# Weight split without a float32 copy, narrower packed operands, and a shorter key norm in a delta-attention and two-FFN kernel

## Chip, core and metric

The kernel runs on one core of a Trainium2 chip. The metric is the device time of one execution in microseconds (us). The engines are PE (TensorE: matmuls, with weight loads listed apart as PEld), DVE (VectorE), ACT (ScalarE), POOL (GpSimd) and SP (SyncE, which here only issues DMAs). Each engine works through its own instructions in order.

## What is computed

A delta-rule attention over 768 steps for 4 x 8 heads of width 48, and after it two feed-forward layers on its 3072 rows of 384 values, with 2048 hidden units each:

```
k_n = k / (np.linalg.norm(k, axis=-1, keepdims=True) + 1e-06)
for t in range(S):
    y[:, :, t] = einsum('bhd,bhde->bhe', q[:, :, t], state)
    v_old = einsum('bhde,bhd->bhe', state, kt)
    state = state + bt * einsum('bhd,bhe->bhde', kt, vt - v_old)
x = y as rows of 384
h = x @ w1_in;  x = maximum(0.01 * h, h) @ w1_out
h = x @ w2_in;  x = (h - tanh(h)) @ w2_out
```

The four weight matrices and all inputs are float32.

## The kernel before

**Numbers.** Matmuls run in float16. A float32 operand is split into two float16 parts, a first part (the rounded value) and a remainder, and a product is made of three matmuls (first by first, first by remainder, remainder by first).

**Attention.** The 768 steps are 12 chunks of 64 (`n` from 0 to 11), two to a unit `u`. For each chunk: keys are normed and split (`keys`, `key_scale`, `key_split`; tile `n` holds the sums of squares and the iteration, `kn` and `KN` the normed keys), transposed on PE (`KTp`), multiplied into the Gram matrix (`Gd`, `AT`); for each unit a triangular inverse is solved column by column on POOL (`X`, `Gd`) and merged on PE (`PM`, `XF`); then states (`R`, `S32`, `SP`) and outputs. `outputs(n)` packs the two heads of a pair beside each other into `Ub` and `Sb`, [128, 2, 8, 128] float16 with 48 columns filled for each head and the last 32 left at zero. Of these a 128-column slice is the stationary operand of each matmul, with `Q` or `P` (64 columns) moving: 24 matmuls with `Ub` and, from the second chunk on, 24 with `Sb` for each of two groups, 576 and 528 in all, each with a weight load of its own.

**Feed-forward.** For each chunk two layers run (`layer(n, 0)`, `layer(n, 1)`), in the order layer 0 of two chunks, then layer 1 of the two. A layer has 8 steps of 18 matmuls into `h_ps` and, three steps later, 18 or 12 matmuls into `o`. Its input `x` is split on DVE by one instruction (`x_split`: ACT makes `xhi`, DVE writes the remainder in place and copies `xhi` in).

**Weights.** They come as float64-wide words. For each of the four matrices (0 is w1_in, 1 w1_out, 2 w2_in, 3 w2_out; tiles `wi` and `wo`) `Weights.convert` assembles float32 on DVE with three bit operations for each pair of 16 blocks of 384 columns, in the place where the split weights will stand; ACT sums the squares (`wacc`), from which one power-of-two scale follows (`sw`). Then `splits` takes each block: ACT makes a scaled float32 copy `wst`, ACT rounds it into the first half of the block, and POOL or DVE (`tt`) subtracts into the second half.

**Order.** The program is written by a planner (`Plan`, `Side`): generators of side work yield the time from which they may go on, by a table of estimated costs, and are stepped between the matmuls of the feed-forward layers; the conversion of weights fills gaps of DVE as it is written. So a change of any step moves instructions of all engines. SP issues every DMA, in the written order, and each DMA waits there until its source is written and its destination is free.

Of the kernel before, what the change touches and what calls it, by code (L numbers as in the profile page):

```python
# [191 lines left out]
def kernel(  # L192
# [29 lines left out]
    N = B * C  # L222
# [5 lines left out]
        return Room(plan, ctx.enter_context(tc.tile_pool(name=name, bufs=bufs, **kw)), bufs)  # L228

    const, wts, live = (room(n, 1) for n in ("const", "wts", "live"))  # L230
    x_p = room("x", NX)
    s_p, g_p = room("s", NSX), room("g", LAG + 1)
    ld_p, q_p = room("ld", 1), room("qld", 1)
    inv_p, pq_p, sm_p = room("inv", 1), room("pq", 2), room("sm", 2)
# [12 lines left out]
    def copy(o, i, scale=1.0):  # L247
        act.activation(out=o, in_=i, func=ACTF.Copy, scale=scale)
# [127 lines left out]
    class Weights:  # L376
# [36 lines left out]
            done.add((self.i, "s"))  # L413

        def splits(self):
            for f in range(NF):
                yield plan.t["act"]
                w = s_p.tile([128, DM], F32, tag="sx", name="wst")
                copy(w, self.f32[:, f], sw[:, self.i:self.i + 1])
                copy(self.dst[:, f, 0], w)  # L420
                tt(self.dst[:, f, 1], w, self.dst[:, f, 0], ALU.subtract, bias())
                done.add((self.i, f))

    def weights():
        wi = [words(w.rearrange("p f c n -> p (f c n)")) for w in WI2]
# [28 lines left out]
    S32 = live.tile([128, NM, D], F32, name="S32")  # L454
    SP = live.tile([128, 2, NM, D], F16, name="SP")
    R = live.tile([128, NG, 2, GM, D], F16, name="R")
    Ub = live.tile([128, 2, GM, 128], F16, name="Ub")
    Sb = live.tile([128, 2, GM, 128], F16, name="Sb")
    HS = [slice(64 * h, 64 * h + 64) for h in range(2)]
    HD = [slice(64 * h, 64 * h + D) for h in range(2)]  # L460
    HL = [slice(64 * h + 32, 64 * h + 64) for h in range(2)]
# [85 lines left out]
    def key_scale(a, y, t):  # L547

        dve.tensor_scalar(out=t, in0=a, scalar1=2.0 ** -100, scalar2=None, op0=ALU.max)
        dve.tensor_scalar(out=y.bitcast(I32), in0=t.bitcast(I32), scalar1=1, scalar2=POW2,  # L550
                          op0=ALU.logical_shift_right, op1=ALU.bitwise_and)
        dve.tensor_scalar(out=t, in0=y, scalar1=2.0 ** 64 / 0.85, scalar2=None, op0=ALU.mult)
        dve.reciprocal(out=y, in_=t)
        for it in range(5):
            if it in (1, 3):
                yield plan.t["dve"]
            dve.tensor_tensor(out=t, in0=y, in1=y, op=ALU.mult)
            dve.scalar_tensor_tensor(out=t, in0=t, scalar=-0.5, in1=a, op0=ALU.mult, op1=ALU.mult)
            dve.scalar_tensor_tensor(out=y, in0=t, scalar=1.5, in1=y, op0=ALU.add, op1=ALU.mult)
        dve.tensor_tensor(out=t, in0=a, in1=y, op=ALU.mult)  # L560
        dve.tensor_scalar(out=t, in0=t, scalar1=1e-6, scalar2=1.0 / KS, op0=ALU.add, op1=ALU.mult)
        dve.reciprocal(out=y, in_=t)
# [315 lines left out]
    def outputs(n):  # L878
        u, s = n // 2, n % 2
        yield from wait(("u", n))  # L880
        yield from wait(("pp", n))
        yield from wait(("x", u))
        Q, P = q_t.pop(n), p_t.pop(n)
        if n > 1:
            yield from wait(("r", n - 3))
            yield from wait(x_owner[-NX])
            x_t[n] = x_tile(("a", n))
        x32 = x_t[n].rearrange("p (t b i) -> p t b i", t=KT, b=B)

        def fill_y(g):  # L890
            halves(Ub, R[:, g], D, D)
            if n > 0:
                halves(Sb, SP[:, :, g * GM:(g + 1) * GM], D, D, HD)

        for g in range(NG):
            qs = qs_t[n, g]
            dve.tensor_scalar(out=qs[:, 4:5], in0=qs[:, 3:4], scalar1=sv_t[u, s][:, 3:4], scalar2=KS, op0=ALU.mult,
                              op1=ALU.mult)
        fill_y(0)
        for g in range(NG):  # L900
            yield Part([Ub, Sb, P[:, g]], 1)
            ps = bank(C)
            for m in range(GM):
                if n > 0:
                    mm3(ps[:, m], Sb, m, (Q[:, g, 0, m], Q[:, g, 1, m]), stop=False)
                mm3(ps[:, m], Ub, m, (P[:, g, 0, m], P[:, g, 1, m]), start=n == 0)
            if g + 1 < NG:
                fill_y(g + 1)
                done.add(("f", n))
            pv = ps.rearrange("p (b t) i -> p t b i", t=HP)  # L910
            xv = x32[:, :, g * 2:g * 2 + 2]
            sc = qs_t.pop((n, g))
            copy(xv[0:96], pv[0:96, 0:KT], sc[0:96, 4:5])
            for t_ in range(KT):
                cp(xv[96:128, t_], pv[32 * t_:32 * t_ + 32, KT], sc[32 * t_:32 * t_ + 32, 4:5])
        done.add(("y", n))
        side.add(to_xa(n), "xa")
# [48 lines left out]
    def h_part(i, x, p, kap):  # L966

        ps = ps_h.tile([128, 2 * N], F32, tag="h", name="h_ps")
        order = [(t, a, b) for t in range(KT) for a, b in ((0, 0), (0, 1), (1, 0))]
        if p == 0:  # L970
            order = [(t, a, 0) for t in range(KT) for a in range(2)] + [(t, 0, 1) for t in range(KT)]
        for j in range(2):
            for n, (t, a, b) in enumerate(order):
                mm(ps[:, j * N:(j + 1) * N], WI[i][:, 2 * p + j, a, t], x[b][:, t], n == 0, n == 3 * KT - 1)
                if n % tune("every") == tune("every") - 1:
                    side.step()
        sx = s_p.tile([128, 2 * N], F32, tag="sx", name="sx")
        if i == 0:
            act.activation(out=sx, in_=ps, func=ACTF.Prelu, scale=C0, alpha=0.01)
        else:  # L980
            act.activation(out=sx, in_=ps, func=ACTF.Tanh, scale=kap[:, 0:1])
            dve.scalar_tensor_tensor(out=sx, in0=sx, scalar=kap[:, 1:2], in1=ps, op0=ALU.mult, op1=ALU.add)
        g = g_p.tile([128, 2, 2 * N], F16, tag="g", name="g")
        if i == 0:
            copy(g[:, 0], sx)
            tt(g[:, 1], sx, g[:, 0], ALU.subtract, bias())
        else:
            split(g[:, 0], g[:, 1], sx, C0)
        return g

    def o_part(i, po, g, p):

        for j in range(2):
            f = 2 * p + j
            first, last = f == 0, f == NF - 1
            gj = g[:, :, j * N:(j + 1) * N]
            for o in range(KT if i == 0 else 2):
                if i == 0 and o == 0 and first:
                    mm(po[0], maskp[:, 0:1].to_broadcast([128, 128]), maskp[:, 0:1].to_broadcast([128, 512]), True, False)
                for n, (a, b) in enumerate(((0, 0), (0, 1), (1, 0))):  # L1000
                    if i == 0:
                        mm(po[o // 2][:, o % 2 * N:o % 2 * N + N], WO[0][:, f, a, o * 128:(o + 1) * 128], gj[:, b],
                           o == 2 and first and n == 0, o > 0 and last and n == 2)
                    else:
                        mm(po[o][:, 0:DM], gj[:, b, o * 128:(o + 1) * 128], WO[1][:, f, a], first and n == 0,
                           last and n == 2)
                side.step()

# [226 lines left out]
```

## Time and profile before

| | us |
|---|---|
| median of 3 runs (1221.56 to 1222.8) | 1221.82 |
| the profiled execution | 1222.18 |
| its span, first to last instruction | 1220.3 |
| PE busy in it | 1013.1 (83%) |
| DVE busy | 736.5 (60%) |
| ACT busy | 634.0 (52%) |
| POOL busy | 509.1 (42%) |

The profiled execution is 0.4 us above the median, and 1.9 us of it lie outside of the span. PE busy is the time in which at least one matmul is under way; a busy engine need not be at its peak.

### The profile page before, as it was taken

The numbers are of one execution on the slowest core, as the hardware profiler recorded it, in microseconds if no ns is written. First come the engines' busy times: TensorE is split into PE (matmuls) and PEld (weight loads), VectorE is DVE, ScalarE is ACT, GpSimd is POOL, SyncE is SP. The second block draws the span as 40 slices with busy tenths as digits, with TensorE's granted clock in tenths as the row PEclk, the third lists the DMA queues.
The fourth block names the chain that finished last, engine by engine and source line by source line (L and its number), as shares of the span: only waits on it lengthen the run. The fifth ranks groups of instructions, "written<-read, shape, count | busy, mean of one in ns | idle before, by whom it ended". The sixth has DMA issues, their size and how long they took to land.

```text
span 1220.3 us, 36850 instructions
## 1 busy us (share of the span) xinstructions
PE 1013.1 (83%) x16216; PEld 831.8 (68%) x16216; DVE 736.5 (60%) x1592; ACT 634.0 (52%) x1409; POOL 509.1 (42%) x635
## 2 busy tenths in 40 slices
PE   0301658898798989989999888899999999999998
PEld 0201547686686878857787766678867888778875
DVE  7997896857567567777755665546753064420243
ACT  3555679695356655645567534435543364333332
POOL 4597446388214872483332682485110321012100
PEclk9999999899898989989999898999999999999999
DMA  9423133100001000000111000001000000000001
GB/s 363 154 84 113 55 106 96 37 24 1 16 23 39 24 22 17 26 23 24 39 32 37 24 1 16 10 8 33 25 10 14 14 12 2 11 17 1 1 1 27
DMA packets 21857, 48.17 MB, mean 39 GB/s; under 512 B 4288, under 2 KB 7360, under 8 KB 21696
## 3 DMA queue, kind: packets, MB, share of 16 engines
q1 hardware_dynamic: 21696, 45.82, 11.9%
q8 instruction: 126, 2.06, 0.7%
q14 instruction: 35, 0.29, 0.1%
HBM read 41.09 MB, written 4.72 MB: 38 GB/s over the span
## 4 chain that ended last, share of the span: by engine, by line
PE 51%; DVE 26%; ACT 11%; POOL 8%; issue 4%; DMA 0%; ACTq 0%; SPq 0%; DVEq 0%; POOLq 0%
PE o L160 21%; PE h_ps L160 19%; PE a_ps L160 11%; DVE n L160 4%; POOL X L160 3%; POOL Gd L160 3%; DVE x L160 2%; ACT g L160 2%; DVE wi L160 2%; DVE g L160 2%; DVE sx L160 2%; DVE wo L160 2%; ACT junk L160 1%; ACT sx L160 1%; DVE X L160 1%
## 5 line engine op out<-in xcount | busy, mean ns | idle before, releaser
L160 PE MATMUL h_ps<-x,wi 128*128 128x256 f16 x3456 | 427.9, 276 | 18.3 <-DVE x L160 12.3
L160 PEld LDWEIGHTS <-wi 128*128 128x128 f16 x3456 | 336.5, 99 | 77.6 <-issue 23.6
L160 PE MATMUL o<-wo,g 128*128 128x384 f16 x1152 | 214.9, 337 | 25.5 <-ACT osb L160 16.0
L160 POOL TENSOR_TENSOR g<-sx,g 128x512 f16<-128x512 f32 x78 | 93.1, 1194 | 311.6 <-ACT g L160 291.6
L160 PE MATMUL o<-g,wo 128*128 128x256 f16 x1728 | 210.6, 275 | 0.0
L160 PEld LDWEIGHTS <-wo 128*128 128x128 f16 x1728 | 167.4, 98 | 32.3 <-issue 10.5
L160 ACT ACTIVATE g<-sx 128x512 f16<-128x512 f32 x192 | 121.0, 630 | 120.2 <-DVE sx L160 117.2
L160 PEld LDWEIGHTS <-g 128*128 128x128 f16 x1152 | 113.7, 100 | 96.0 <-issue 36.0
L160 DVE SCALAR_TENSOR_TENSOR sx<-sx,kap,h_ps 128x512 f32<-128x512 f32 x96 | 71.2, 741 | 92.9 <-ACT sx L160 92.6
L160 POOL TENSOR_TENSOR Gd<-X 128x30 f32<-128x30 f32 (+9 forms) x180 | 110.8, 616 | 33.3 <-DVE X L160 19.5
L160 POOL TENSOR_TENSOR X<-X,Gd 128x30 f32<-128x30 f32 (+9 forms) x180 | 114.8, 638 | 14.1
L160 DVE SCALAR_TENSOR_TENSOR g<-sx,g 128x512 f16<-128x512 f32 x96 | 74.3, 774 | 67.4 <-ACT g L160 67.4
L160 ACT ACTIVATE sx<-h_ps,kap 128x512 f32<-128x512 f32 x96 | 65.4, 681 | 81.6 <-PE h_ps L160 71.3
L160 ACT ACTIVATE sx<-h_ps 128x512 f32<-128x512 f32 x96 | 56.5, 589 | 93.9 <-PE h_ps L160 87.6
L160 PEld LDWEIGHTS <-KTp 64*64 64x64 f16 x3360 | 66.2, 118 | 36.4 <-issue 34.4
L160 POOL TENSOR_TENSOR P<-P,maskp 128x1024 f16<-128x1024 f16 x24 | 52.6, 2196 | 61.4 <-DVE P L160 58.2
L160 PE MATMUL a_ps<-ab,ones 128*128 128x1 bf16 x124 | 11.7, 168 | 75.3 <-DVE ab L160 73.4
L160 PEld LDWEIGHTS <-KN 64*64 64x64 f16 x1824 | 37.5, 120 | 39.7 <-issue 35.7
L160 PE MATMUL a_ps<-Q,Sb 128*128 128x64 f16 x528 | 35.7, 199 | 13.2 <-DVE Sb L160 13.2
L160 PEld LDWEIGHTS <-ones 128*128 128x128 bf16 x124 | 7.8, 102 | 54.0 <-DVE ab L160 50.0
L160 PE MATMUL a_ps<-Q,KTp 64*64 64x64 f16 x1152 | 25.4, 201 | 23.1 <-ACT Q L160 20.2
L160 ACT ACTIVATE x<-a_ps,qs 32x128 f32<-32x128 f32 (+1 forms) x57 | 25.5, 447 | 31.4 <-PE a_ps L160 28.2
(161 smaller groups left out, 1533.1 us busy)
## 6 DMA issues: line engine op xcount, KB each, us to landing
wo<-in_w_in_dram SPq DMA_DIRECT2D x32, 384.0 KB, 6.1
qf<-in_q_dram SPq DMA_DIRECT2D x24, 256.0 KB, 2.6
wi<-in_w_out_dram SPq DMA_DIRECT2D x14, 384.0 KB, 7.8
kf<-in_k_dram SPq DMA_DIRECT2D x12, 384.0 KB, 4.1
vf<-in_v_dram SPq DMA_DIRECT2D x12, 384.0 KB, 4.1
out_dram<-osb SPq DMA_DIRECT2D x48, 96.0 KB, 2.2
wo<-in_w_out_dram SPq DMA_DIRECT2D x8, 384.0 KB, 3.8
stage<-in_w_out_dram SPq DMA_DIRECT2D x8, 384.0 KB, 3.8
```

The source lines that it names most:

```text
L160: return getattr(self.eng[eng], op)(*args, **kw)
```

## The change

Four edits. `splits` works on two blocks at a time: ACT rounds the scaled float32 values straight into a tile `wh` of its own (two buffers), DVE makes the remainders from the float32 values, the scale and `wh`, and writes them into the first half of the blocks, over float32 values that it has read; then a DMA, issued by SP, moves `wh` into the second half. As first parts and remainders change places, the feed-forward matmuls take `1 - a` where they took `a`. `key_scale` begins from a guess made by a shift, a product and a sum on the bits of the norm, and iterates three times, where it began from a power of two and a reciprocal and iterated five times. `Ub` and `Sb` are 96 columns wide for each head pair, where they were 128, and their matmuls write 96 rows.

```diff
-    x_p = room("x", NX)
+    x_p, wh_p = room("x", NX), room("wh", 2)
...
         def splits(self):
-            for f in range(NF):
+
+            s_ = sw[:, self.i:self.i + 1]
+            for f in range(0, NF, 2):
                 yield plan.t["act"]
-                w = s_p.tile([128, DM], F32, tag="sx", name="wst")
-                copy(w, self.f32[:, f], sw[:, self.i:self.i + 1])
-                copy(self.dst[:, f, 0], w)
-                tt(self.dst[:, f, 1], w, self.dst[:, f, 0], ALU.subtract, bias())
-                done.add((self.i, f))
+                w = wh_p.tile([128, 2, DM], F16, name="wh")
+                copy(w, self.f32[:, f:f + 2], s_)
+                lo_of(self.dst[:, f:f + 2, 0], self.f32[:, f:f + 2], s_, w)
+                sp.dma_start(out=self.dst[:, f:f + 2, 1], in_=w)
+                done.update((self.i, f + i) for i in range(2))
...
-    Ub = live.tile([128, 2, GM, 128], F16, name="Ub")
-    Sb = live.tile([128, 2, GM, 128], F16, name="Sb")
+    Ub = live.tile([128, 2, GM, 2 * D], F16, name="Ub")
+    Sb = live.tile([128, 2, GM, 2 * D], F16, name="Sb")
...
         dve.tensor_scalar(out=t, in0=a, scalar1=2.0 ** -100, scalar2=None, op0=ALU.max)
-        dve.tensor_scalar(out=y.bitcast(I32), in0=t.bitcast(I32), scalar1=1, scalar2=POW2,
-                          op0=ALU.logical_shift_right, op1=ALU.bitwise_and)
-        dve.tensor_scalar(out=t, in0=y, scalar1=2.0 ** 64 / 0.85, scalar2=None, op0=ALU.mult)
-        dve.reciprocal(out=y, in_=t)
-        for it in range(5):
-            if it in (1, 3):
+        dve.tensor_scalar(out=t.bitcast(I32), in0=t.bitcast(I32), scalar1=1, scalar2=None,
+                          op0=ALU.logical_shift_right)
+        dve.tensor_scalar(out=y.bitcast(I32), in0=t.bitcast(I32), scalar1=-1.0, scalar2=float(0x5F375A00),
+                          op0=ALU.mult, op1=ALU.add)
+        for it in range(3):
+            if it == 1:
                 yield plan.t["dve"]
...
                 if n > 0:
-                    mm3(ps[:, m], Sb, m, (Q[:, g, 0, m], Q[:, g, 1, m]), stop=False)
-                mm3(ps[:, m], Ub, m, (P[:, g, 0, m], P[:, g, 1, m]), start=n == 0)
+                    mm3(ps[0:2 * D, m], Sb, m, (Q[:, g, 0, m], Q[:, g, 1, m]), stop=False)
+                mm3(ps[0:2 * D, m], Ub, m, (P[:, g, 0, m], P[:, g, 1, m]), start=n == 0)
...
-                mm(ps[:, j * N:(j + 1) * N], WI[i][:, 2 * p + j, a, t], x[b][:, t], n == 0, n == 3 * KT - 1)
+                mm(ps[:, j * N:(j + 1) * N], WI[i][:, 2 * p + j, 1 - a, t], x[b][:, t], n == 0, n == 3 * KT - 1)
```

In the whole program ACT loses 128 instructions of 384 columns and gains 32 of 768; POOL loses all of its 49 subtractions on weights and DVE its 15; DVE gains 32 remainders of 768 columns; SP gains 32 DMAs of 192 KB. DVE loses 7 instructions in each of 11 key scales.

The planner then moves work of DVE. Before, this stands on DVE around the split of the input of the first feed-forward layer (`x<-x,sxs,xhi`; `wo_107` is the tile of w2_out and w2_in's load space, `stage` more load space, `sxs` the scale of x):

```order
L160 CAST KTp_116<-a_ps 128x512
L160 SCALAR_TENSOR_TENSOR wo_107<-wo_107 128x768 x2
L160 TENSOR_SCALAR wo_107<-stage 128x768
L160 SCALAR_TENSOR_TENSOR wo_107<-stage,wo_107 128x768
L160 SCALAR_TENSOR_TENSOR x<-x,sxs,xhi 128x768
L160 COPY x<-xhi 128x768
```

And this now (`wi_108` is w2_in, `wo_109` w1_out, `wo_110` what was `wo_107`):

```order
L160 TENSOR_SCALAR wi_108<-wo_110 128x768
L160 SCALAR_TENSOR_TENSOR wi_108<-wo_110,wi_108 128x768
L160 SCALAR_TENSOR_TENSOR wo_109<-wo_109,sw,wh 128x2x384
L160 CAST ab<-sc 128x1
L160 SCALAR_TENSOR_TENSOR x<-x,sxs,xhi 128x768
L160 COPY x<-xhi 128x768
```

So before that split the conversion of w2_out (matrix 3) had already begun; now the one of w2_in (matrix 2) isn't quite finished there. Of all that stands on DVE ahead of it, 275 instructions before and 226 now, there have gone behind it: 14 instructions of the conversion of w2_out, the norm and split of the third key chunk (22 instructions on `n`, three on `kn` and `KN`), three `KTp` casts; 9 subtractions on weights are gone, and 16 remainders are there instead.

Behind it, the same engine holds this before, between the splits of the inputs of the first and the second chunk (`Gd` and `AT` are the Gram matrix of the third chunk, `Q` and `P` the queries and products of the second):

```order
L160 TENSOR_SCALAR wo_107<-stage 128x768
L160 SCALAR_TENSOR_TENSOR wo_107<-stage,wo_107 128x768
L160 SCALAR_TENSOR_TENSOR Q<-qf,qs,Q 128x512
L160 SCALAR_TENSOR_TENSOR P<-a_ps,P 128x512
L160 TENSOR_TENSOR wo_106<-wst,wo_106 128x384
```

And now:

```order
L160 SCALAR_TENSOR_TENSOR wi_108<-wi_108,sw,wh 128x2x384
L160 TENSOR_TENSOR kn<-kf,n_915 128x384 x2
L160 TENSOR_TENSOR KN_115<-kn,KN_115 128x8x48
L160 CAST ab<-qs 128x1
L160 TENSOR_SCALAR wo_110<-wo_110 128x768
```

So the third chunk's keys, the whole conversion of w2_out but its scale, and the 8 remainders of w2_in now stand between the two splits.

## Rows read from the trace of the kernel before

**Rows 1.** The page, part 1: busy us, share, instructions.

```profile
PE 1013.1 (83%) x16216; PEld 831.8 (68%) x16216; DVE 736.5 (60%) x1592; ACT 634.0 (52%) x1409; POOL 509.1 (42%) x635
```

**Rows 2.** Busy time by stretch: stretch, length, each engine's busy us, clock, DMA.

```profile
0.00:182.00 182.00, 49.63 (x1544) 46.29 (x1545) 157.72 (x277) 103.81 (x235) 110.63 (x133) 1.00 0.42 147
182.00:234.00 52.00, 43.51 (x597) 36.90 (x596) 39.38 (x87) 41.57 (x102) 25.50 (x22) 0.97 0.25 77
234.00:269.00 35.00, 33.34 (x502) 28.27 (x502) 18.86 (x53) 31.05 (x79) 25.61 (x31) 0.95 0.07 22
269.00:1220.00 951.00, 886.59 (x13578) 720.35 (x13575) 520.56 (x1178) 457.55 (x995) 347.35 (x450) 0.96 0.07 18
```

**Rows 3.** Timeline, PE and DVE: start, us, what, idle before and releaser.

```profile
179.65 1.01 DVE L160 SCALAR_TENSOR_TENSOR x<-x,sxs,xhi 128x768 f16<-128x768 f32 x1
...
181.70 0.58 PE L160 MATMUL h_ps<-x,wi 128*128 128x256 f16 x2 [5.57 <-DVE x L160]
...
233.54 1.01 DVE L160 SCALAR_TENSOR_TENSOR x<-x,sxs,xhi 128x768 f16<-128x768 f32 x1
...
268.88 0.48 DVE L160 TENSOR_TENSOR kap<-sxs,sw 128x1 f32<-128x1 f32 x1
```

**Rows 4.** Groups by form, whole run: busy us, mean ns, idle before.

```profile
L160 ACT ACTIVATE wst<-wi,sw 128x384 f32<-128x384 f32 x32 | 19.2, 601 | 1.4 <-DVE sw L160 1.3
L160 ACT ACTIVATE wi<-wst 128x384 f16<-128x384 f32 x32 | 16.7, 523 | 1.0
L160 POOL TENSOR_TENSOR wo<-wst,wo 128x384 f16<-128x384 f32 x26 | 25.9, 996 | 24.8 <-ACT wo L160 22.9 <-DVE ab L160 1.6
L160 ACT ACTIVATE xhi<-x,sxs 128x768 f16<-128x768 f32 x24 | 22.2, 924 | 4.9 <-DVE sxs L160 3.0 <-DVE ab L160 1.7 <-DVE n L160 0.2
L160 DVE SCALAR_TENSOR_TENSOR x<-x,sxs,xhi 128x768 f16<-128x768 f32 x24 | 28.8, 1200 | 18.7 <-ACT xhi L160 18.3
```

**Rows 5.** The same view, DVE alone, first 269 us.

```profile
L160 DVE SCALAR_TENSOR_TENSOR wo<-wo 128x768 int32<-128x768 int32 x8 | 10.0, 1248 | 0.2
...
L160 DVE TENSOR_TENSOR wi<-wst,wi 128x384 f16<-128x384 f32 x9 | 9.5, 1058 | 2.1 <-ACT wi L160 2.1
...
L160 DVE SCALAR_TENSOR_TENSOR n<-n 128x16 f32<-128x16 f32 x20 | 5.4, 270 | 0.7
...
L160 DVE SCALAR_TENSOR_TENSOR x<-x,sxs,xhi 128x768 f16<-128x768 f32 x3 | 3.0, 1012 | 4.4 <-ACT xhi L160 4.4
...
L160 DVE TENSOR_SCALAR wo<-wo 128x768 int32<-128x768 int32 x4 | 2.3, 576 | 0.0
```

**Rows 6.** Timeline of POOL, inside the first inverse and at its end.

```profile
63.19 1.57 POOL L160 TENSOR_TENSOR wi<-wst,wi 128x384 f16<-128x384 f32 x1
...
109.68 0.32 POOL L160 TENSOR_SCALAR X<-bt 128x32 f32<-128x32 f32 x1
```

**Rows 7.** Weight loads by tile: ns shortest, median, longest; first and last start.

```profile
L160 PEld LDWEIGHTS <-Ub x576: 95/98/133, 145.9 to 1019.7; 128*128 128x128 f16 x192
...
L160 PEld LDWEIGHTS <-KTp x3360: 102/110/156, 31.3 to 996.6; 64*64 64x64 f16 x198
```

**Rows 8.** Timeline of PE: one run at the low clock, one at the high.

```profile
120.83 5.30 PE L160 MATMUL a_ps<-X,AT 64*64 64x32 f16 x192 [1.12 <-DVE X L160]
...
151.07 1.46 PE L160 MATMUL a_ps<-P,Ub 128*128 128x64 f16 x24 [3.73 <-DVE Ub L160]
152.46 0.25 PE L160 MATMUL a_ps<-SP,KTp 64*64 64x48 f16 x2
...
219.55 0.25 PE L160 MATMUL a_ps<-Q,Sb 128*128 128x64 f16 x3
...
220.95 1.47 PE L160 MATMUL o<-g,wo 128*128 128x256 f16 x12
```

**Rows 9.** Groups by form, whole run: the matmuls on the packed tiles.

```profile
L160 PE MATMUL a_ps<-P,Ub 128*128 128x64 f16 x576 | 38.6, 203 | 3.7 <-DVE Ub L160 3.7
...
L160 PE MATMUL a_ps<-Q,Sb 128*128 128x64 f16 x528 | 35.7, 199 | 13.2 <-DVE Sb L160 13.2
```

**Rows 10.** DMA issues: KB each, median us from issue to landing.

```profile
qf<-in_q_dram SPq DMA_DIRECT2D x24, 256.0 KB, 2.6
```

**Rows 11.** The chain that ended last, 400 to 600 us, by line.

```profile
by line: PE o L160 16.3%; PE h_ps L160 14.8%; PE a_ps L160 13.7%; DVE n L160 6.8%; DVE x L160 5.3%; DVE g L160 4.1%; ACT g L160 3.8%; issue 3.7%; DVE sx L160 3.5%; ACT junk L160 2.4%; DVE X L160 2.0%; DVE kn L160 1.9%; ACT sx L160 1.5%; DVE
```

More of the change, by code (lines that the diff above doesn't have):

```diff
@@ L1001, in o_part @@
                     if i == 0:
-                        mm(po[o // 2][:, o % 2 * N:o % 2 * N + N], WO[0][:, f, a, o * 128:(o + 1) * 128], gj[:, b],
+                        mm(po[o // 2][:, o % 2 * N:o % 2 * N + N], WO[0][:, f, 1 - a, o * 128:(o + 1) * 128], gj[:, b],
                            o == 2 and first and n == 0, o > 0 and last and n == 2)
                     else:
-                        mm(po[o][:, 0:DM], gj[:, b, o * 128:(o + 1) * 128], WO[1][:, f, a], first and n == 0,
+                        mm(po[o][:, 0:DM], gj[:, b, o * 128:(o + 1) * 128], WO[1][:, f, 1 - a], first and n == 0,
                            last and n == 2)
```

## Prediction

> **What bounds the kernel now.** I read the page's busy times first: PE is busy for 83% of the span, no other engine for more than 60% [rows 1]. Then the same by stretch, which says where the other 17% lie [rows 2]. In the first 182 us PE works for 49.6 us and DVE for 157.7 of 182: here DVE is the bound, and PE waits for the attention of the first chunk. From 182 to 234 PE works 43.5 of 52 us, from 234 to 269 33.3 of 35. From 269 us to the end it works 886.6 of 951 us, so some 64 us of waits are scattered there. Two bounds then: DVE until the feed-forward layers run, PE's own work after it. The timeline gives three marks for the first part [rows 3]: the first chunk's input is split on DVE at 179.65 us and PE's first `h_ps` matmul starts at 181.70; the second chunk's input is split at 233.54; `kap`, with which the second layer begins, stands at 268.88. What I forecast is how these marks move, and what PE's work after them costs.
>
> **The weight split.** Each pair of blocks cost ACT 2 x (0.601 + 0.523) = 2.25 us and two subtractions of about 1.0 us on POOL or 1.06 us on DVE [rows 4, 5]. Now it costs ACT one instruction as `xhi`, 0.92 us, and DVE one as the split of `x`, 1.01 us early in the run and 1.20 in the mean of all [rows 4, 5]. Over 32 pairs ACT is spared 42 us and POOL 49 us; DVE gains 32 x 1.0 to 1.2, 32 to 38 us, and is spared 15 subtractions, 15 us at the most. ACT and POOL bound nothing there, with one exception: POOL's chain for the first inverse holds four such subtractions (one of 1.57 us at 63.19) before its end at 109.68 [rows 6], about 5 us.
>
> The 32 new DMAs move 192 KB each. The nearest row is the 256 KB load of `qf`, 2.6 us to landing [rows 10]; a move within SBUF is not in the trace, so I take 2 to 4 us. Two buffers of `wh` let the third rounding start when the first DMA has landed. Between two remainders DVE has 3 us or more of other work in the written order nearly everywhere, so this hides; if a DMA took twice that, a pair would still be split in about 4 us. On SP each DMA waits for its remainder, and loads of `qf`, `kf` and `vf` are queued behind it; they had waited on SP for their buffers before as well, and I take nothing for that, 0 to 3 us as the bound.
>
> **The first mark.** Ahead of the first split DVE loses, by the two orders: 14 instructions of the conversion of w2_out (nine of 1.25, five of 0.58: 14 us), 22 on `n` at 0.27 and three on `kn` and `KN` (7 us), 9 subtractions (9 us), 7 small ones of the first keys (1.5 us) and a few casts (3 us, an estimate): 35 us [rows 5]. It gains 16 remainders, 16 to 19 us. The balance is 16 to 19 us less on the engine that bounds this stretch, and the inverse's chain on POOL ends about 10 us earlier as well (5 us of subtractions, the rest by an earlier start), so it doesn't hold this back. I put the first split at 163 us, 17 earlier, and the first `h_ps` at 165.
>
> **The second mark.** This gain isn't kept, since what went behind the first split lies before the second. In this stretch DVE gets the 14 us of w2_out, some 5 us of keys, the casts and the 8 remainders of w2_in (8 to 10 us), less two subtractions and what the shorter iteration spares: about 24 us more. Of its 52 us it was busy 39.4 [rows 2], so 6 of the 12.6 idle us can take some of it, and POOL no longer works on weights beside it: 4 us, as DVE's instructions here are up to a fifth longer in the mean over the run than early on (1.20 against 1.01 for the same form) [rows 4, 5]. So 17 - (24 - 6 - 4) = 3 us of the gain is left at the second mark, where PE now waits some 15 us for the second chunk. From there to `kap` PE has the same 33 us of work [rows 2]. Take 3.5 us for this whole part; bounds: +6 (the remainders at 1.20, no idle time used) and -15 (the gain of the first mark nearly kept).
>
> **The key norms.** Each of ten later key scales loses 7 of 22 instructions on `n`, at 0.27 us nearly 2 us. The chain of waits passes through `n` for 6.8% of the 200 us from 400 to 600 [rows 11], 13.6 us, so a third of this, over the 500 us in which keys are made, is about 10 us at the most. Behind it in DVE's queue stand `sx` and `g` of the feed-forward, which PE waits for; but PE is then often held by its next cause. I take 5 us, bounds 0 and 10.
>
> **The narrower packed operands.** This looks like housekeeping, and is the largest term. Each of 1104 matmuls on `Ub` and `Sb` loads its own stationary operand. What a load costs PE is seen where the moving operand is short [rows 8]. `X,AT` moves 32 columns and loads 64, for two heads side by side: 192 matmuls in 5.3 us, 27 ns each, 55 for a pair. At the clock's lower level, 1.2 GHz (the pace says so, at the start of the trace, where the granted clock reads 1.00), 32 columns take 27 ns and 64 take 53, so the load of 64 columns, one for each clock, sets this pace. `P,Ub` in the same stretch moves 64 columns and loads 128: 24 in 1.39 us from 151.07 to 152.46, 58 ns each, where a load of 128 at one column a clock would take 107. At the higher level the 48 matmuls from 219.55 to 220.95 come every 29 ns, again the 64 columns that move. So the load of the full 128 is faster than one column a clock and stays hidden, and a load of 64 isn't. The records of single loads agree: between the two levels a 128-column load grows from 98 to 133 ns, a 64-column one from 110 to 156, more for half the columns [rows 7].
>
> A load of 96 columns isn't in the trace. Bounds: it stays hidden, 0; or it runs one column a clock, as the loads of 64 do: 96 / 2.4 = 40 ns at the higher level, 13.3 ns more than the 26.7 that move, and 26.7 more at the lower. About a seventh of these matmuls are at the lower level (an estimate from the means of 203 and 199 ns, which the slower ones raise) [rows 9], so 15.3 ns each. I take the second, since a row of 64 on part of the array is the only narrow load there is. 1104 x 15.3 ns = 16.9 us; 144 of them fall in the first two chunks, where PE waits anyway, so 14.7 us on the path. Bounds 0 and 20.
>
> The Trainium skill speaks to just this place: its page "TensorE: Matmul & The Clock Gate", section "Weight-path perf modes — Fast Weight Load (FWL) and DoubleRow", says that the fast load of weights is on only when there are 128 of them and the type isn't float32, so 96 columns would lose it. By that rule the sum is the one taken here; without it this term is 0 and the sum that of the third rival. No run here shows a 96-column load yet.
>
> **The sum.** The profiled execution took 1222.2 us: 1222.2 - 3.5 - 5 + 14.7 = 1228.4. The median lies 0.4 below the profiled time, so 1228.
>
> **Rivals.** *The start keeps its gain.* If POOL's absence speeds DVE more, or the deferred conversion finds idle time, 15 us stay of the 17 at the second mark: 1222 - 15 - 5 + 15 = 1217, faster. For it: DVE was idle for 12.6 of 52 and 16 of 35 us there; against it: 24 us more work lies between the two marks. It decides at about 9 us kept. *DVE gives back more than it gained.* With remainders at 1.2 us, a wait for each second `wh`, and the key chains of the third chunk later, `kap` comes 6 us later and the short keys bring nothing: 1222 + 6 + 15 = 1243. *The narrow load stays hidden.* Then 1222 - 3.5 - 5 = 1213, and the edit of `Ub` and `Sb` does nothing. Against it is the pace of `X,AT`.
>
> **How the numbers follow.** The forecast gets 0.57, with its own range 1218 to 1238; the first rival 0.15, the slower one 0.18, the hidden load 0.10. The predicted time is 1228. The range of 1211 to 1241 takes in both faster rivals and half of the slower one. A measurement of this kernel can tell about 0.2%, 2.4 us: faster is below 1219.4, slower above 1224.3. The first rival puts 0.12 below and the hidden load 0.09, the forecast's lower end 0.06: 0.27. Within: 0.11 of the forecast, 0.03 and 0.01 of these: 0.16 with a little of the slower one. Slower: 0.57.
>
> **What would show it.** In the changed profile: the first `h_ps` near 165 us, the second chunk's split near 230, `kap` near 265; a wait of PE for DVE between 205 and 230; 48 matmuls on `Sb` and `Ub` taking about 2.0 us at the higher level, not 1.4; single loads of these tiles longer than 110 ns; PE's busy time about 15 us higher. The forecast is wrong if those 48 still take 1.4 us, or if `kap` lies before 258 or after 275 us.

## The result, and the profile after

The changed kernel took 1230.41 us in the median of 4 runs (1228.96 to 1231.62), the kernel before 1221.69 beside it: 1.0069 times as long, 95% interval 1.0052 to 1.0087, so 8.7 us slower. The profiled execution has a span of 1228.7 us. The forecast was 1228.

Busy time of the engines in the changed kernel, the line that answers to [rows 1]:

```profile
PE 1030.5 (84%) x16216; PEld 851.6 (69%) x16216; DVE 736.3 (60%) x1555; ACT 594.6 (48%) x1305; POOL 453.4 (37%) x571
```

ACT is spared 39 us and POOL 56; DVE's sum hasn't moved; PE is busy for 17.4 us more with the same 16216 matmuls. The same by stretch (length; busy us of PE, its loads, DVE, ACT, POOL; clock; DMA), for [rows 2]:

```profile
0.00:182.00 182.00, 68.59 (x1754) 61.60 (x1755) 153.43 (x283) 87.24 (x186) 85.65 (x108) 0.65 0.47 160
182.00:234.00 52.00, 33.85 (x492) 28.99 (x491) 43.94 (x100) 33.16 (x84) 13.04 (x10) 0.80 0.31 102
234.00:269.00 35.00, 32.16 (x473) 27.75 (x471) 26.11 (x42) 23.56 (x63) 26.72 (x32) 1.00 0.19 59
269.00:1220.00 951.00, 892.51 (x13487) 731.45 (x13485) 512.16 (x1132) 450.06 (x971) 328.00 (x424) 0.96 0.07 18
```

PE works 19 us more than before in the first stretch and 9.7 less in the second: the first chunk's layer starts sooner, then PE waits. The marks of the timeline (start, us, what; in brackets the idle time before it and what ended it), for [rows 3]:

```profile
154.34 1.01 DVE L160 SCALAR_TENSOR_TENSOR x<-x,sxs,xhi 128x768 f16<-128x768 f32 x1
...
155.80 4.45 PE L160 MATMUL h_ps<-x,wi 128*128 128x256 f16 x24 [1.12 <-DVE x L160]
...
216.57 0.24 PE L160 MATMUL a_ps<-ab,ones 128*128 128x1 bf16 x2 [8.38 <-DVE ab L160]
...
222.24 1.02 DVE L160 SCALAR_TENSOR_TENSOR x<-x,sxs,xhi 128x768 f16<-128x768 f32 x1 [2.04 <-ACT xhi L160]
...
223.71 1.44 PE L160 MATMUL h_ps<-x,wi 128*128 128x256 f16 x6 [5.96 <-DVE x L160]
...
262.83 0.51 DVE L160 TENSOR_TENSOR kap<-sxs,sw 128x1 f32<-128x1 f32 x1
```

The first split is 25.3 us earlier than before, the second 11.3, `kap` 6.05. PE's two waits at 216.57 and 223.71 are 14.3 us together: here most of the gain of the first mark goes. From the second split to `kap` the changed kernel takes 40.6 us, before 35.3, and so 5 more go: PE is busy there for 36.3 us and was for 33.2. From `kap` to the end of the span the changed kernel needs 965.9 us, the one before 951.4. So 6 us were won ahead of `kap` and 14.5 lost behind it.

What was lost behind it shows in the groups of the matmuls on the packed operands (busy us, mean ns of one), in the records of single loads (ns shortest, median, longest) and in PE's timeline, for [rows 7 to 9]:

```profile
L160 PE MATMUL a_ps<-P,Ub 128*96 128x64 f16 x576 | 55.7, 220 | 3.0 <-DVE Ub L160 3.0
L160 PE MATMUL a_ps<-Q,Sb 128*96 128x64 f16 x528 | 51.3, 216 | 9.8 <-DVE Sb L160 9.7
```

```profile
L160 PEld LDWEIGHTS <-Ub x576: 125/125/196, 129.1 to 1028.7; 128*96 128x96 f16 x192
```

```profile
197.69 0.28 PE L160 MATMUL a_ps<-Q,Sb 128*96 128x64 f16 x3
197.80 0.30 PE L160 MATMUL a_ps<-P,Ub 128*96 128x64 f16 x3
...
199.69 0.30 PE L160 MATMUL a_ps<-P,Ub 128*96 128x64 f16 x3
199.83 0.38 PE L160 MATMUL o<-g,wo 128*128 128x256 f16 x2
```

The two groups are busy for 107.0 us, before 74.3. The 48 matmuls from 197.69 to 199.83 come every 44.6 ns, before every 29.2. The shortest record of a load is 125 ns, before 95, for a quarter less columns.

The DMAs that move the first parts (KB each, median us from issue to landing):

```profile
wi<-wh SPq DMA_DIRECT2D x16, 192.0 KB, 2.3
wo<-wh SPq DMA_DIRECT2D x16, 192.0 KB, 2.3
```

### The profile page after: what moved, and what is told of

The parts are those of the page before. It is cut to its first block, busy times and chain, and to the rows that moved or that the text cites. A ratio compares the mean times of both kernels' runs of the same rounds, so it can differ in the third digit from the quotient of the medians.

```text
span 1228.7 us, 36692 instructions
## 1 busy us (share of the span) xinstructions
PE 1030.5 (84%) x16216; PEld 851.6 (69%) x16216; DVE 736.3 (60%) x1555; ACT 594.6 (48%) x1305; POOL 453.4 (37%) x571
## 4 chain that ended last, share of the span: by engine, by line
PE 52%; DVE 22%; POOL 13%; ACT 9%; issue 4%; ACTq 0%; DVEq 0%; POOLq 0%
PE o L160 21%; PE h_ps L160 19%; PE a_ps L160 12%; POOL X L160 6%; POOL Gd L160 5%; DVE n L160 3%; DVE wi L160 2%; DVE x L160 2%; DVE wo L160 2%; DVE g L160 2%; ACT junk L160 1%; DVE Ub L160 1%; ACT g L160 1%; DVE sx L160 1%; DVE p L160 1%
## 5 line engine op out<-in xcount | busy, mean ns | idle before, releaser
L160 PEld LDWEIGHTS <-wi 128*128 128x128 f16 x3456 | 337.1, 100 | 77.5 <-issue 19.1
L160 PE MATMUL o<-wo,g 128*128 128x384 f16 x1152 | 208.7, 331 | 17.4 <-ACT osb L160 10.6
L160 POOL TENSOR_TENSOR g<-sx,g 128x512 f16<-128x512 f32 x68 | 82.2, 1209 | 335.9 <-ACT g L160 326.0
L160 POOL TENSOR_TENSOR X<-X,Gd 128x30 f32<-128x30 f32 (+9 forms) x180 | 120.4, 669 | 14.1
L160 DVE SCALAR_TENSOR_TENSOR g<-sx,g 128x512 f16<-128x512 f32 x96 | 70.5, 734 | 67.0 <-ACT g L160 67.0
L160 PEld LDWEIGHTS <-KTp 64*64 64x64 f16 x3360 | 69.2, 122 | 15.3 <-issue 14.1
L160 PEld LDWEIGHTS <-KN 64*64 64x64 f16 x1824 | 36.3, 117 | 45.3 <-issue 36.3
L160 PE MATMUL a_ps<-Q,Sb 128*96 128x64 f16 x528 | 51.3, 216 | 9.8 <-DVE Sb L160 9.7
L160 PE MATMUL a_ps<-P,Ub 128*96 128x64 f16 x576 | 55.7, 220 | 3.0 <-DVE Ub L160 3.0
L160 PEld LDWEIGHTS <-Sb 128*96 128x96 f16 x528 | 41.5, 133 | 13.3 <-DVE Sb L160 12.5
```

Of the source, the lines that this page charges most:

```text
L160: return getattr(self.eng[eng], op)(*args, **kw)
```

## The experiments

Twelve kernels ran, each beside the kernel before on the same chip in the same set. A difference in us below is that of a run's median to the median of before in its set. The question was first which of the change's parts cost the 8.7 us, and then whether the two others did what the prediction says.

### The width of the loads

The kernel before, with narrower loads from tiles that stay 128 wide; no other instruction moves.

```diff
-  mm3(ps[:, m], Sb, m, (Q[:, g, 0, m], Q[:, g, 1, m]), stop=False)
+  mm3(ps[0:2 * D, m], Sb[:, :, :, 0:2 * D], m, (Q[:, g, 0, m], Q[:, g, 1, m]), stop=False)
   (and the same for Ub and P; in the second run 0:112 for 0:2 * D)
```

> The kernel before, in which the 1104 matmuls on Ub and Sb load only the 96 filled columns of each 128 and write 96 rows; tiles, order and every other instruction stay. Theory (a load of 96 columns takes one column a clock and sets the pace): 48 such matmuls take 2.1 us at the higher level, not 1.4, so each costs 15.4 ns more; 1104 x 15.4 = 17.0 us, of which 2 to 3 us fall where PE waits anyway, so 1236 to 1239 us with PE busy some 17 us longer. Rival (the start's reordering made the changed kernel slower, the load is hidden): 1221.7, within 0.2%.

1235.59 us, +14.4 (ratio 1.0118, 1.0101 to 1.0134).

> The kernel before, with 112 of 128 columns loaded for each matmul on Ub and Sb, all else the same. Theory (one column a clock for every load that is not the full 128): 112 columns take 46.7 ns at the higher level against 40 for 96, so the pace is 51 ns where 96 gave 44.6, and the loss is 22 ns x 1104 = 24 us, at most 28 with a seventh of them at the lower level: 1244 to 1249 us. First rival (any load short of 128 pays one fixed price): the same time as with 96 columns, about 1238. Second rival (the price shrinks as the load comes closer to 128): below that, 1222 to 1236.

1246.84 us, +25.6 (1.021, 1.0189 to 1.0231). The groups with 112 columns:

```profile
L160 PE MATMUL a_ps<-P,Ub 128*112 128x64 f16 x576 | 61.7, 226 | 2.8 <-DVE Ub L160 2.8
L160 PE MATMUL a_ps<-Q,Sb 128*112 128x64 f16 x528 | 56.4, 220 | 12.5 <-DVE Sb L160 12.5
```

and in its timeline the change of the clock from the higher to the lower level within one row of matmuls:

```profile
214.82 0.32 PE L160 MATMUL a_ps<-Q,Sb 128*112 128x64 f16 x3
214.98 0.32 PE L160 MATMUL a_ps<-P,Ub 128*112 128x64 f16 x3
...
216.51 0.47 PE L160 MATMUL a_ps<-P,Ub 128*112 128x64 f16 x3
216.79 0.47 PE L160 MATMUL a_ps<-Q,Sb 128*112 128x64 f16 x3
```

Three matmuls take 0.155 us, so 52 ns each, and later 0.28 us, 93 ns each. At one column a clock 112 columns take 46.7 ns at 2.4 GHz and 93.3 at 1.2. With 96 columns the two paces are 45 and 80 ns (40 and 80 by the clock). With 128 columns they are 29 and 53, where the 64 columns that move take 26.7 and 53.3. The lower paces of 96 and of 128 columns, from the run before this one and from the kernel before:

```profile
215.18 0.43 PE L160 MATMUL a_ps<-Q,Sb 128*96 128x64 f16 x3
215.42 0.43 PE L160 MATMUL a_ps<-P,Ub 128*96 128x64 f16 x3
```

```profile
214.96 0.35 PE L160 MATMUL a_ps<-Q,Sb 128*128 128x64 f16 x3
215.12 0.35 PE L160 MATMUL a_ps<-P,Ub 128*128 128x64 f16 x3
```

So a load of 96 or 112 columns sets the pace at one column a clock, with about 5 ns on top at the higher level, and one of 128 doesn't. The two rivals, a fixed price and a price that shrinks towards 128, are both out: 16 columns more cost 11 us more, and the last 16 give 26 us back. The edits also write fewer rows of the result (96 and 112 for 128); as 112 rows are slower than 96 and than 128, the rows aren't the cause.

The other direction, in the changed kernel:

```diff
+    UF = live.tile([128, 2, GM * 2 * D + 32], F16, name="Ub")     (SF the same)
+    Ub = UF[:, :, 0:GM * 2 * D].rearrange("p c (m n) -> p c m n", m=GM)
-                mm3(ps[0:2 * D, m], Ub, m, ...)
+                mm3(ps[:, m], UF, slice(m * 2 * D, m * 2 * D + 128), ...)
```

> The changed kernel, whose Ub and Sb keep the pitch of 96 columns for a head pair, but each matmul loads 128: the 96 of its pair and the first 32 of the next one (32 columns of zero stand behind the last). The 32 extra rows of the result are read by nobody. Theory: the 48 matmuls take 1.4 us again, and the time falls by what the narrow loads cost, 14 to 17 us, to 1213 to 1217, faster than the kernel before; the marks of the start stay where they are in the changed kernel (first split 154, second 222, kap 263). Rival (the loss comes from DVE's order after kap): 1228 to 1231, no change from the changed kernel.

1214.62 us, -6.6 (0.9949, 0.9936 to 0.9961): 15.3 us below the changed kernel and below the kernel before. The marks are those of the changed kernel to 0.4 us (154.41, 222.30, 263.18), and the 48 matmuls take 1.39 us again:

```profile
197.06 0.25 PE L160 MATMUL a_ps<-Q,Sb 128*128 128x64 f16 x3
...
198.37 0.25 PE L160 MATMUL a_ps<-P,Ub 128*128 128x64 f16 x3
198.45 0.49 PE L160 MATMUL o<-g,wo 128*128 128x256 f16 x3
```

The narrow loads cost 14 to 15 us in either kernel. Of the tiles' smaller size nothing has to be given up: the pitch stays at 96 columns, only each load reaches over its neighbour.

### The split alone, and the key norm alone

Split without the short key norm, with overlapping loads:

> The kernel before with the weight split alone: the key scale iterates five times from a power of two as before, and Ub and Sb are loaded 128 columns at a time, as in the run with overlapping loads. Theory (the split moves kap some 6 us earlier and the short key norm brings about 5 more): 1216 to 1220. Rival 1 (all of the gain of the start comes from the split, the keys bring nothing): within 2 us of the run with overlapping loads and the short key norm. Rival 2 (without the short key norm DVE gives back all that it gained): 1221 or more.

1253.67 us, +32.4 (1.0268, 1.025 to 1.0286). Rival 2 has the direction, but neither it nor the theory has the size. The marks are 178.07, 240.46 and 282.71: without the short key norm the first split is hardly earlier than before (179.65), and `kap` is 14 us later. Key norm without the split:

> The kernel before with the short key norm alone (7 instructions fewer in each of 11 key scales); the planner writes its order anew. By the prediction's term 5 us less: 1216.5, bounds 1211 to 1221. Theory (what the short key norm changes is mostly the order that the planner writes, not the 77 instructions): the time differs by more than 4 us, to either side, from that of the next kernel, which has the same instructions in the old order. Rival (the instructions themselves): both within 2 us of each other.

1235.88 us, +13.6 (1.0117, 1.0103 to 1.0131). Each of the two alone makes the kernel slower; both together, with full loads, make it faster. That isn't a sum of prices, so the next three runs hold the order fixed. They let the planner count the old instructions and leave some out, or add some behind its back:

```diff
 (order of before, or of the split alone: reciprocal and iterations 4 and 5 counted but not written)
+            plan.ghost = it >= 3
             dve.tensor_tensor(out=t, in0=y, in1=y, op=ALU.mult)
...
 (order of split and short norm: the same seven written but not counted)
+        raw = plan.eng["dve"]
+        raw.reciprocal(out=t, in_=y)
+        for it in range(2):
+            raw.tensor_tensor(out=t, in0=y, in1=y, op=ALU.mult)
...
```

> The kernel before with the short key norm, whose 77 left-out instructions are still counted in the planner's times, so that all others stand in the same order as before. This is the price of the instructions alone: by the prediction 5 us less, bounds 0 and 10, so 1211 to 1221.5. Rival (the 39 us between the run with the split alone and the one with split and short key norm are these instructions): 20 us less or more, 1201 and below.

1208.27 us, -14.0 (0.9887, 0.9872 to 0.9902): the fastest of all, faster than both kernels. Marks 176.65, 230.39, 265.58.

> The run with overlapping loads (split, short key norm, 128 columns; 1214.6 us) with 7 more instructions in each key scale, a reciprocal and two more iterations, of which the planner knows nothing: the order of all others stays. Theory (order): the 77 instructions cost what the prediction took, 5 us, at most 12: 1217 to 1227, and the first split of x stays before 160. Rival (the instructions themselves made the split alone so slow): 1245 to 1254.

1233.29 us, +11.0 (1.0097, 1.008 to 1.0114), so 17.7 more than without the seven in each key scale. Marks 156.16, 225.33, 268.34.

> The run with the split alone (1253.7 us) in its own order, without the 77 instructions, which the planner still counts. Theory (order): it stays slow, 1240 to 1250, with the first split near 175 and kap near 275. Rival (instructions): 1213 to 1220, the time of the run with overlapping loads and the short key norm.

1240.84 us, +18.6 (1.0146, 1.0125 to 1.0166), so 13.8 less than with them. Marks 175.96, 238.91, 279.25.

In three orders the 77 instructions are worth 14.0, 17.7 and 13.8 us. They were given 5, and at most 10 or 12. And the order is worth more than they are: the key norm alone has nearly the same instructions as the run of 1208.27 (36789 against 36773), written in the order (and with the choice of DVE or POOL) that the planner makes of it, and takes 27.6 us more. The early first mark of the changed kernel isn't the split's either. With the split alone that mark stands at 178.07, with 77 instructions fewer in that order at 175.96, and only in the order that the planner makes for both together at 154.41.

Why the 77 weigh so much is seen in the chain of work that ended last, from 269 us to the end, by line: first the kernel before, then the run with the old order and the short norm.

```profile
by line: PE o L160 26.9%; PE h_ps L160 24.3%; PE a_ps L160 13.0%; DVE n L160 3.6%; issue 2.6%; DVE g L160 2.6%; ACT g L160 2.5%; DVE sx L160 2.4%; DVE x L160 2.0%; ACT sx L160 1.4%; ACT junk L160 1.4%; DVE Sb L160 1.1%; DVE Ub L160 1.1%; PO
```

```profile
by line: PE o L165 27.0%; PE h_ps L165 24.1%; PE a_ps L165 13.4%; POOL X L165 3.0%; issue 2.5%; POOL Gd L165 2.5%; DVE g L165 2.2%; ACT g L165 2.0%; DVE x L165 2.0%; DVE sx L165 1.9%; DVE n L165 1.6%; DVE Sb L165 1.4%; ACT junk L165 1.2%; D
```

`DVE n` is 3.6% of 951 us, 34 us, and then 1.6% of 939 us, 15 us. About 9 of these 19 us came out as time (951.4 us from `kap` to the end, then 942.6); 3.3 us more came ahead of `kap`. The prediction's 0.27 us for one of them is a mean of unlike cases, too: in the kernel before, 59 of the 100 `SCALAR_TENSOR_TENSOR` steps on `n` run beside no instruction of POOL and take 0.17 to 0.18 us; the 41 others have a median of 0.47 and take up to 2.12.

### The split in the old order

```diff
 (order of before with the short key norm; the old three instructions counted, these written)
+                wh = wh_p.tile([128, DM], F16, name="wh")
+                eng["act"].activation(out=wh, in_=self.f32[:, f], func=ACTF.Copy, scale=s_)
+                eng["dve"].scalar_tensor_tensor(out=self.dst[:, f, 0], in0=self.f32[:, f], scalar=s_, in1=wh, ...)
+                eng["sp"].dma_start(out=self.dst[:, f, 1], in_=wh)
```

> The order of the kernel before with the 77 key instructions left out (1208.3 us), and in it the new weight split by single blocks, at the places where the old one stood: ACT rounds 384 columns into a tile wh of three buffers, DVE makes the remainder in place, a DMA of 96 KB moves the first part in; the planner goes on counting the old instructions, so that nothing else moves. This is the price of the split without any new order. Theory (DVE bounds the start, ACT and POOL don't): 64 remainders on DVE of some 0.55 us, 35 us, for 15 subtractions of 1.06, 16 us, so the first split comes 5 to 15 us later, kap 0 to 12 us later, and the time is 1208 to 1221. Rival (the prediction's reading: less on POOL and an earlier end of the inverse's chain more than make up for it): 1195 to 1206.

1219.45 us, -3.2 (0.9968, 0.9957 to 0.9978), so 10.8 more than the same order with the old split; marks 188.01, 242.62, 278.73. The time is the theory's, with `kap` a little later than it allowed (13.2 us), but its reason, more work on DVE, is the smaller part. Up to the first split, 11.4 us later than in the same order with the old one, DVE is busy for 2.7 us more and idle for 8.7 us more (old split, new split; DVE's busy time is the third of the five):

```profile
0.00:176.65 176.65, 49.36 (x1542) 46.08 (x1543) 152.89 (x260) 102.26 (x229) 109.54 (x132) 1.00 0.43 151
```

```profile
0.00:188.01 188.01, 49.40 (x1542) 45.95 (x1543) 155.56 (x288) 84.19 (x192) 76.33 (x104) 1.00 0.47 161
```

DVE waits in the first 269 us for ACT's rounding (us in all, times, longest),

```profile
DVE wi L437 <- ACT wh L436: 16.8, 14, 1.7
DVE wo L437 <- ACT wh L436: 9.2, 9, 2.9
```

26.0 us, where POOL had done nearly all of this waiting before (46.5 us, and DVE 3.1). In the changed kernel these waits are 6.9 us. So the last run took the wait away by rounding one block ahead:

```diff
-                eng["act"].activation(out=wh, in_=self.f32[:, f], func=ACTF.Copy, scale=s_)
+                for j in range(0 if f == 0 else f + 1, min(f + 2, NF)):
+                    t = wh_p.tile([128, DM], F16, name="wh")
+                    eng["act"].activation(out=t, in_=self.f32[:, j], func=ACTF.Copy, scale=s_)
+                    ahead.append(t)
+                wh = ahead.pop(0)
```

> The run with the split in the old order (1219.5 us; DVE waited 26.0 us there for ACT's wh), but ACT rounds each block one block ahead, so that its remainder finds wh ready; all else stays. Theory (a part of the 11 us that the split costs there is this wait): DVE's waits for wh fall under 8 us, the first split of x comes 5 to 9 us earlier than 188, and the time falls to 1208 to 1215. Rival (DVE's work on 64 remainders is the price): 1217 to 1222.

1223.43 us, +1.8 (1.0017, 1.0006 to 1.0028): slower than with the wait, by 5.0. DVE's waits for `wh` fell from 26.0 to 2.7 us as expected, and came back on ACT in the same stretch:

```profile
ACT wh L438 <- DMA wo<-wh: 19.7, 6, 5.9
ACT wh L438 <- DMA wi<-wh: 19.3, 6, 7.8
```

A block that is held ahead keeps a buffer of `wh`, and with three buffers for two matrices at a time ACT stood before a DMA that hadn't landed, and that itself had to wait on SP until DVE had written the remainder (SP's waits for remainders of `wo` rose from 53.4 to 72.8 us). In ACT's queue behind it were steps of the attention (for example the rounding of `R`), on which DVE waited 4.5 us at 179.15. So ahead of the first split the price in this order is for the most part waits, as the windows show, but no run took them away; what would be left without them stays open.

### The DMA

DVE copies `wh` in place of the DMA, in the order of the run with overlapping loads:

```diff
-                sp.dma_start(out=self.dst[:, f:f + 2, 1], in_=w)
+                dve.tensor_copy(out=self.dst[:, f:f + 2, 1], in_=w)     (counted by the planner as the DMA)
```

> The run with overlapping loads (1214.6 us) in the same order, but DVE copies each wh into the second half of its blocks where a DMA did. Theory (the DMA is hidden and spares DVE a copy in the stretch that it bounds): 32 copies of 768 columns, 0.3 to 0.8 us each, put 10 to 25 us on DVE; kap comes 5 to 15 us later: 1219 to 1230. Rival (the two transports with their waits cost as much as a copy): 1214.6, within 2 us.

1223.43 us, +0.8 by the medians (the ratio, 0.9998, 0.9983 to 1.0012, tells no difference from before), so 7.4 more than with the DMA by the medians and 6 by the ratios; `kap` comes at 269.12, 5.9 later. The copies (busy us, mean ns):

```profile
L162 DVE COPY wi<-wh 128x768 f16<-128x768 f16 x16 | 9.5, 596 | 0.5
L162 DVE COPY wo<-wh 128x768 f16<-128x768 f16 x16 | 7.9, 492 | 0.5
```

17.4 us of copies, all but the last five ahead of 269 us, moved `kap` by 5.9 and the end by 7.4. The DMA is hidden in the changed kernel: ACT waits 0.3 us for it in the first 269 us.

### The deferred conversion of w2_out

```diff
         r = (wo[1][nh // 2:] * 2)[0:NF // 2] + words(stage) * (NF // 4)
         b = Weights(3, w2_out, WO[1], r)
+        yield from wait(("n", 1))
         yield from b.convert()
```

> The run with overlapping loads (1214.6 us), with the conversion of w2_out held back until the third key chunk's norm is done, so that less of it stands on DVE between the first and the second split of x (76 instructions between them, 103 before). Theory (this work between the splits is what gives the gain of the first mark back): the second split comes near 213, 9 us earlier, PE waits less there; kap comes earlier by up to 6 us if the conversion finds room later: 1208 to 1215. Rival (the conversion is on the path wherever it stands): second split earlier, kap and the time the same or later, 1214 to 1222.

1215.74 us, -6.9 (0.9939, 0.9923 to 0.9955), within 0.3 us of the run with overlapping loads by the medians, so no gain clear of the noise. The second split stands at 206.69 (222.30 there) and `kap` at 249.56, 13.6 us earlier, and nearly all of it is lost again in one wait of PE:

```profile
296.73 3.92 PE L160 MATMUL o<-wo,g 128*128 128x384 f16 x12 [12.25 <-DMA wo<-wh]
```

The first matmul on w2_out waits until its last step, the DMA, has brought the first parts in. So the conversion between the two splits is what gives the first mark's gain back, as predicted, but moving it away only moved the wait, to the place where PE first needs w2_out.

## Why the prediction was right, point by point

**The sum came out, with two terms wrong in opposite directions.** The forecast was -3.5 for split and marks, -5 for the key norms, +14.7 for the loads: +6.2, measured +8.7.

**The narrower operands: right, in cause and size.** +14.7 was forecast; +14.4 in the old kernel, +15.3 in the changed one. The hidden load, 0, is excluded. 112 columns, which the prediction didn't consider, show that the reading "one column a clock below 128" holds between its two known points, 64 and 128. The pace of 48 matmuls was 2.14 us for "about 2.0": 44.6 ns each, a further 4.6 beyond the 40. The runs agree with the rule that the prediction cited from the Trainium skill (page "TensorE: Matmul & The Clock Gate", section "Weight-path perf modes — Fast Weight Load (FWL) and DoubleRow"): loads of 96 and 112 columns set the pace, 45 and 52 ns, and those of 128 left it at 29. The same page of the Trainium skill gives a load of P columns P / 1.2 ns in its section "LDWEIGHTS (loading the stationary operand)", and no clock level with it; that fits the 80 and 93 ns of 96 and 112 columns at the lower level, not the 45 and 52 at the higher, and here the measurement decides.

**The key norms: right in sign, mis-sized.** The step that failed is "a third of this ... is about 10 us at the most", and with it "I take 5 us, bounds 0 and 10". The measured 14 to 18 us lie outside these bounds. Two things were missed. The first key scales, ahead of `kap`, count too: 3.3 us in the old order, 5.2 in the new. And the halving for "PE is then often held by its next cause" had no row: the whole chain from 269 us holds 34 us of `n`, a third of which is 11, and 9 came out.

**The weight split: a gain where the old order shows a loss.** "Take 3.5 us for this whole part" was put down as a gain over the old order. With short key norm and full loads on both sides, the split with the order that comes with it costs 7.4 us against that order (1214.62, -6.6, against 1208.27, -14.0), and 10.8 where that order is kept. Against the order that the planner makes for the short key norm without the split (1235.88, +13.6) it gains 20.2 us: apart from an order the split has no price. That the sum came within 2.5 us of the measured +8.7 was in part luck, since two misses of 9 and 11 us cancelled. "ACT and POOL bound nothing there" failed for ACT in the old order, where DVE waits 26.0 us for it, and nearly held in the changed kernel, 6.9 us. The other single steps were right: 36 us of remainders on DVE (19.1 for `wi` at 1.19 us) for 32 to 38; ACT and POOL 39 and 56 us less for 42 and 49; DMAs of 2.3 us, hidden; the inverse's chain on POOL ends at 101.03 for "about 10 us earlier" than 109.68. The marks came as read from the order, but earlier: 154 for 163, 222 for 230, 263 for 265, with some 15 us of waits of PE between 205 and 230. The first mark's 9 us are a term that the prediction left out: up to the first split DVE is busy for 129.9 us, 155.4 before, 25.5 less where the listed instructions make 17. The instructions that stayed got shorter too, as POOL no longer subtracts weights beside them. The same 16 steps of the conversions of w1_in and w2_in take, before and after:

```profile
L160 DVE TENSOR_SCALAR wi<-wo 128x768 int32<-128x768 int32 x16 | 12.4, 773 | 0.0
```

```profile
L160 DVE TENSOR_SCALAR wi<-wo 128x768 int32<-128x768 int32 x16 | 9.0, 560 | 0.0
```

In the old order, with all other instructions in place, they fall from 12.4 to 9.5 us when the split leaves POOL; and in the kernel before one of them takes 0.54 us beside an idle POOL and the next 1.27 beside a subtraction:

```profile
128.86 0.54 DVE L160 TENSOR_SCALAR wi<-wo 128x768 int32<-128x768 int32 x1
...
131.03 1.12 POOL L160 TENSOR_TENSOR wi<-wst,wi 128x384 f16<-128x384 f32 x1 [3.36 <-ACT wi L160]
131.30 1.27 DVE L160 TENSOR_SCALAR wi<-wo 128x768 int32<-128x768 int32 x1
```

The prediction allowed for this in the second stretch alone (4 us). What went wrong is the credit. The early first mark was set against the split, but in the run with the split alone it hardly moved; it belongs to the order that the planner makes when the key norm is short too. With the split alone 260 instructions of DVE, 150.6 us, stand ahead of the first split of `x`, in the changed kernel 225, 129.9 us: among the 35 more are eight steps of the conversion of w2_out, five remainders of w2_in and seven steps on `n`. And behind `kap` the prediction let only key norms and loads act: by these, -8.8 and +14 to 15, the stretch should have been 6 us longer; it was 14.5. With overlapping loads it is 950.4 us, where the old order with the short norm has 942.6. These 8 us are waits, since PE is busy for 881.8 us in the one stretch and 882.8 in the other. In the changed kernel's order PE waits longer for DVE's `ab`, `sx` and `x` (7.2 us for 3.7), and less for ACT's `osb` (10.6 for 19.4); us in all, times and longest, with overlapping loads and with the old order:

```profile
PE a_ps L160 <- DVE ab L160: 10.0, 4, 5.5
PE h_ps L160 <- DVE sx L160: 6.9, 5, 2.3
```

```profile
PE a_ps L165 <- DVE ab L165: 2.9, 4, 1.5
PE h_ps L165 <- DVE sx L165: 1.2, 2, 0.8
```

They are put down to the order of the later chunks; no run tested that alone.

**The rivals.** *The start keeps its gain*: in part. At the second mark 11.3 of 25.3 us were left, more than the 9 at which the prediction let it decide, but 6 at `kap`, and the kernel became slower. *DVE gives back more than it gained*: not here, but with the split alone just this happens, `kap` 14 us later and +32 us; the short key norm, with the order that comes with it, keeps the changed kernel from it. *The narrow load stays hidden*: excluded. The prediction's reading of the pair `X,AT` holds in the trace of before: the matmuls of the two heads start within 3 ns of each other, a pair every 53 ns.

## What to carry to other kernels

Don't narrow a stationary operand below the full 128 columns to save memory where the moving operand is as short as here (64 columns): let the load reach over its neighbour's columns and ignore the extra rows. Where a planner writes the order, an edit has two prices, its own work and the new order; a kernel that goes on counting the old instructions, but writes the new ones, separates them, and its time can also be the best of all (here 1208 against 1222 and 1230). Before an engine is relieved, look at which other engine's instructions get shorter by it. When a sum of terms comes out, test the terms one by one before believing them: here -14 and +7 stood where -5 and -3.5 had been put down.

## What the runs showed of the hardware

**A load of 112 columns is slower than one of 128, by far**: 52 against 29 ns for each matmul at the higher clock, 93 against 53 at the lower, 25.6 us over 1104 loads.

**The clock column says little where PE is mostly idle.** The kernel before and the one with 96-column loads have the same order and, up to there, the same timeline. For the first 182 us the mean granted clock reads 1.00 in the one [rows 2] and 0.62 in the other:

```profile
0.00:182.00 182.00, 50.42 (x1544) 47.15 (x1545) 157.72 (x277) 103.81 (x235) 110.56 (x133) 0.62 0.42 147
```

while the same 192 matmuls take 5.30 us in both, the pace of the lower level (before in [rows 8], now with 96-column loads):

```profile
120.81 5.30 PE L160 MATMUL a_ps<-X,AT 64*64 64x32 f16 x192 [1.14 <-DVE X L160]
```

The trace of before has no entry of the clock ahead of 187 us, the other one has its first at 35.7, and the view counts what lies ahead of a first entry as 1.00. The changed kernel's first entry stands at 29.5 us. So its lower mean clock, 0.911 for 0.970, is no sign of a loss, and the kernel before bears this out: beside the split in the old order 8 of its runs read 0.967 to 0.971 with a median of 1222.1 us, and 15 read 0.906 to 0.916 with 1223.0. The pace of matmuls tells the level.

**A DMA from one tile to another takes nearly as long for half the bytes**: 2.3 us to landing for 192 KB, 2.0 and 1.9 for 96 KB (2.5 and 1.9 in the run that rounds ahead). Where buffers are few, the way through SP's queue and the landing together are the price: ACT's 39 us of waits there were 3.3 us in the mean and up to 7.8.

**An instruction of DVE can take over twice as long while POOL works**: in the kernel before 0.54 to 0.56 us for the steps `wi<-wo` beside an idle POOL, 1.27 beside its subtractions on weights, 0.54 to 0.86 beside its steps on `X` and `Gd`; 0.18 us for the steps on `n`, and up to 2.12.
